# Retention and two FFNs on one core: load order of the first units, the place of float64 conversions, and two turns for background work

## The chip, the cores and the metric

One core of one Trainium2 chip runs the whole program in one launch. The metric is device microseconds of one execution; a smaller time is better. The engines are named as the profile names them: PE is TensorE (matmuls; PEld its weight loads), DVE is VectorE, ACT is ScalarE, POOL is GpSimd and SP is SyncE, which here only issues DMAs. An entry such as L456 is a line of the kernel before; in the changed kernel the same lines stand five lower in the first stage, seven lower in the next and nine lower in the last.

## The reference

The input is q, k and v (4 batches, 8 heads, 768 positions, 64 wide, float32) and two pairs of weights in float64. What is computed is a retention layer and two feed-forward networks on its 3072 tokens of width 512:

```python
for t in range(S):
    state = gamma * state + einsum('bhd,bhe->bhde', k[:, :, t], v[:, :, t])
    y[:, :, t] = scale * einsum('bhd,bhde->bhe', q[:, :, t], state)
x = y as (3072, 512)
h = x @ w_in                            # 512 -> 2048, float64 weights
x = (h * (1 / (1 + exp(-1.702 * h)))) @ w_out
h = x @ w_in2
x = (max(h, 0) ** 2) @ w_out2
```

## The kernel before, in words

**Attention stage.** The retention is cut into 24 units (4 batches by 6 chunks of 128 positions, all 8 heads). The loop at L564 to L575 runs one unit u per pass. `scores(u)` puts 16 small matmuls on PE (L456, tile `sc`), which DVE masks into `pt` (`masked`, L465); a scaled copy `vs` of v is made by POOL (L475, for u below 6 and each third unit) or by ACT (L480). `outputs(u-1)` then puts three groups on PE: `yp` (L508, needs `pt` and `vs`), `dp` (L519, the update of the state) and a second part of `yp` (L530, from the state `st`, which ACT copies at L524). DVE scales `yp` into the token blocks `x` or `xout` (`scaled`, L543, L547, L550). The tile `sc` has one buffer, so the scores of a unit wait until DVE has masked the unit before. Units 0 to 3 make block 0, whose operands `hl` ACT and DVE split at L491 and L492.

**Loads of units.** SP loads each unit in two halves of 512 KB (`load_unit`, L447): q and k laid out in pairs (columns 0 to 1024, read by the scores) and k and v by token (columns 1024 to 2048, read by `vs` and `dp`; called "kv" here). Five units have buffers. The order of the first loads is written out at L555 to L562; later, unit u+4 is asked for at the end of pass u. The small tables `tab_sb` and `ytab` lie between the first loads.

**Conversion of weights.** The first network's weights come as float64 slices of 512 KB, 32 in all. POOL's queue loads a slice into `raw` (`cv_load`, L119). ACT scales its two words (`scale_words`, called by `cv_a`; L124, L125). DVE joins them to a float32 (`join`, L129 and L134) and rounds (`round_up`, L142); ACT copies the high part (L157) and DVE subtracts for the low part (L162). `cv_step` is called once in each pass of the attention loop. It places one scaling if a slice has been asked for and fewer than two scaled ones lie ready, and a conversion in those passes that `CVU` lists; `masked` and `scaled` are put between its steps. The raw loads begin in the pass whose number the last argument of `cv_step` gives. By the end of the attention stage 9 slices are converted; the other 23 follow in the first block of the next stage.

**First network, first four blocks** (`NSTD` = 4 blocks of 512 tokens). Each block has 16 steps f; a step has `up(n, f)` (12 matmuls, L595 to L597) and `down(n, f - 2)` (12 matmuls, L626 to L628). ACT makes `gs` (L602) and its high part `gh` (L603), DVE the low part `gl` (L607), which `down` reads two steps later.

**Makers.** Once all 32 slices are converted, DVE and ACT also make the sums of weights that a seven-product form of matrix multiplication needs later. `make_first` and `make_second` are generators; `make_second` converts the 32 slices `raw2_n` of the second network (loaded by ACT's queue, L247), sums them into `w32_n`, lets ACT cast them to `wq_n` (L353) and writes each by a POOL DMA of 896 KB to `kw` in DRAM (L316). `background(us)` gives them a turn: it first drains ACT's pending pieces (`acts`), then advances the maker until the given microseconds (`BG` in the first network, `BGUP` later, with what is left over) are used up, or until it must wait for a piece of ACT.

**The rest.** The last two blocks of the first network and all of the second run as seven products (L769). SP fetches their weights as tiles `r` of 256 KB from `kw`, into 8 slots, one for each 6 matmuls. POOL loads the next operands `xb` in four DMAs of 512 KB (L641) halfway through each `up2`. The order on each engine is the order in which the program emits the work.

Of the kernel before, what the change touches and what calls it, by code (L numbers as in the profile page):

```python
# [26 lines left out]
NF = DFF // P  # L27
# [2 lines left out]
UPB = TB // P  # L30
WA = 8
LOOK = 2
WARM = 10
UNITS = 5
XHELD = 4
NL = NT // (2 * TB)
# [4 lines left out]
NSTD = 4  # L41
SLOTS = 8
EARLY = 2
BG = 4.8
CVU = (5, 8, 11, 14, 17, 20, 21, 22, 23)
RAWS = 5
BGUP = 1.8

# [9 lines left out]
def tile_retention_then_two_ffns(  # L58
# [38 lines left out]
    order = []  # L97
# [5 lines left out]
            order.append((f, 1))  # L103
    wpool = {f: wa_p for f in range(WA)}
    ws = {}
    cv = {"load": 0, "a": 0, "b": 0, "pool": None, "ahead": 3}
    cvt = {}

    def cv_load():
        n = cv["load"]  # L110
        if n == len(order):
            return
        if n >= cv["b"] + cv["ahead"]:
            return
        cv["load"] += 1
        f, s = order[n]
        raw = cv_p.tile([P, 512, 2], U32, tag="raw", name=f"raw{n}", bufs=RAWS)
        src = w1[f, :, s * 512:(s + 1) * 512].bitcast(U32)
        nc.gpsimd.dma_start(out=raw, in_=src.rearrange("p (c t) -> p c t", t=2))  # L119
        cvt[n] = raw  # L120

    def scale_words(hm, raw):

        nc.scalar.mul(hm, raw[:, :, 1].bitcast(F32), 2.0 ** -112)  # L124
        nc.scalar.mul(raw[:, :, 0], raw[:, :, 0], 2.0 ** -29)  # L125

    def join(out, hb):

        v.tensor_scalar(  # L129
            out=out, in0=hb, scalar1=3, scalar2=0x7FFFFFFF,  # L130
            op0=ALU.logical_shift_left, op1=ALU.bitwise_and,
        )
        yield
        v.scalar_tensor_tensor(  # L134
            out=out, in0=hb, scalar=0x80000000, in1=out, op0=ALU.bitwise_and, op1=ALU.bitwise_or
        )
        yield
# [6 lines left out]
    def cv_a():  # L144

        n = cv["a"]
        if n == min(cv["load"], cv["b"] + 2):
            return
        cv["a"] += 1
        scale_words(cvt[n][:, :, 1].bitcast(F32), cvt[n])  # L150

# [2 lines left out]
    def cv_high():  # L154
        if held:
            w, hm, key = held[0]
            nc.scalar.copy(out=w[:, :, 0], in_=hm.rearrange("p (k c) -> p k c", c=P))  # L157

    def cv_low():
        if held:  # L160
            w, hm, key = held.popleft()
            v.tensor_tensor(  # L162
                out=w[:, :, 1], in0=hm.rearrange("p (k c) -> p k c", c=P), in1=w[:, :, 0], op=ALU.subtract
            )
            ws[key] = w

    def cv_step(limit=len(order), f1=None, f2=None, load=True):

        n, ready = cv["b"], cv["a"]
        if cv["pool"] is not None and limit is not None:  # L170
            cv_a()
        cv_high()
        if limit is None or n >= min(limit, ready):
            for f in (f1, f2):
                if f is not None:
                    f()
            cv_low()
        else:
            cv["b"] += 1
            raw = cvt.pop(n)  # L180
            key = order[n]
            hm = cv_p.tile([P, 512], F32, tag="hm", name=f"hm{n}")
            w = wpool[key[0]].tile([P, 4, 2, P], F32R, tag=f"w{key[1]}", name=f"w{n}")
            steps = join(hm.bitcast(U32), raw[:, :, 1])
            next(steps)
            if f1 is not None:
                f1()
            next(steps)
            round_up(hm, raw)
            if f2 is not None:  # L190
                f2()
            cv_low()
            held.append((w, hm, key))
        if limit is None:
            return
        if cv["pool"] is None:
            cv_a()
        if load:
            cv_load()
            cv_load()  # L200
# [177 lines left out]
    def background(us):  # L378

        credit[0] += us  # L380
        while acts:
            acts.popleft()()
        while credit[0] > 0:
            c = next(maker, None)
            if c is None:
                credit[0] = min(credit[0], 3.0)
                return
            credit[0] -= c
# [21 lines left out]
    with tc.manual_schedule():  # L410

        with (
# [20 lines left out]
            warm = aps.tile([P, 2, NP, P], F32, tag="sc", name="warm", bufs=1)  # L433
            for i in range(WARM):
                nc.tensor.matmul(warm[:, 0, :, :], warm_sb[:, 0:P], warm_sb, start=True, stop=True)
# [5 lines left out]
            def load_unit(u, parts=(0, 1024, 2048)):  # L441
                if u >= NU:
                    return
                if u not in units:
                    units[u] = att.tile([P, 2048], F32, tag="unit", name=f"unit{u}", bufs=UNITS)
                for a, z in zip(parts, parts[1:]):
                    nc.sync.dma_start(out=units[u][:, a:z], in_=qkv[u, :, a:z])  # L447
# [106 lines left out]

            load_unit(0, (0, 512, 1024))  # L555
            nc.sync.dma_start(out=tab_sb, in_=tab)
            load_unit(1, (0, 1024))
            load_unit(0, (1024, 2048))
            load_unit(1, (1024, 2048))
            nc.sync.dma_start(out=ytab_sb[0], in_=ytab)  # L560
            for u in range(2, UNITS):
                load_unit(u)  # L562
# [1 line left out]
            for u in range(NU + 1):  # L564
                masked = scores(u) if u < NU else None
                split_0()
                scaled = outputs(u - 1) if u > 0 else None
                if 0 < u < CPB:
                    for p in range(NP):
                        nc.scalar.mul(ytab_sb[u][:, p, :], ytab_sb[0][:, p, :], ystep_sb[:, u, p:p + 1])  # L570
                if u == 18:
                    cv["ahead"] = RAWS
                cv_step(2 * WA if u in CVU else 0, masked, scaled, u >= 2)
                if u > 0:
                    load_unit(u + UNITS - 1)  # L575

# [9 lines left out]

        gs = {}
        acc = {}

        def up(n, f):  # L590
            hi, lo = weights(f, 0)
            hp = hp_p.tile([P, TB], F32, tag="h", name=f"h{n}_{f}")
            for k in range(KD):
                xh, xl = hl[n][k]
                nc.tensor.matmul(hp, lo[:, k], xh, start=(k == 0), stop=False)  # L595
                nc.tensor.matmul(hp, hi[:, k], xh, start=False, stop=False)  # L596
                nc.tensor.matmul(hp, hi[:, k], xl, start=False, stop=(k == KD - 1))  # L597
            g = g_p.tile([P, TB], F32, tag="gs", name=f"gs{n}_{f}", bufs=1)
            gh = g_p.tile([P, TB], F32R, tag="gh", name=f"gh{n}_{f}")
            gl = g_p.tile([P, TB], F32R, tag="gl", name=f"gl{n}_{f}")  # L600

            nc.scalar.activation(out=g, in_=hp, func=ACTF.Gelu_apprx_sigmoid)  # L602
            nc.scalar.copy(out=gh, in_=g)  # L603
            gs[n, f] = (gh, gl)

            def low():
                v.tensor_tensor(out=gl, in0=g, in1=gh, op=ALU.subtract)  # L607

            if n == 0 and cv["b"] < len(order):
                cv_step(len(order), None, low)  # L610
                if f % 4 < 3:
                    cv_step()
            else:
                low()
                if f < NF - 1:

                    background(BG if n < NSTD - 1 or f < 5 else BG - 1.6)

        def down(n, f):
            hi, lo = weights(f, 1)  # L620
# [9 lines left out]
        def finish(n):  # L630
            a = acc.pop(n)
            t = block_tiles(f"y{n}")
            for e in range(KD):
                (nc.scalar.copy if e % 2 else v.tensor_copy)(out=t[e // 2][:, e % 2], in_=a[e])
            for i in range(2):
                nc.gpsimd.dma_start(out=ykept[n][:, 2 * i:2 * i + 2], in_=t[i])
# [83 lines left out]
        for n in range(NSTD):  # L720
            for f in range(NF):
                up(n, f)
                if f >= LOOK:
                    down(n, f - LOOK)
                elif n > 0 and f == 0:
                    down(n - 1, NF - 1)
                    finish(n - 1)
                if f == 2 and XHELD - 2 <= n < NSTD - 2:
                    xs[n + 2] = load_block(f"x{n + 2}", xkept[n + 2])
                if n == 0 and f in (2, 3):  # L730
                    j = XHELD + f - 2
                    nc.gpsimd.dma_start(out=xkept[j], in_=xout[j])
                if n == NSTD - 1:
                    if f == 3:
                        gen = x_operands(*x_loads(*blocks[0]))
                    if f >= 5:
                        next(gen, None)
                    if f == NF - 3:
                        fetch()
            down(n, NF - 2)  # L740
            if n + 1 < NSTD:
                split_x(n + 1, xs.pop(n + 1))
# [324 lines left out]
```

## Time and profile before

| what | us |
|---|---|
| median of 3 runs | 1060.19 (1059.11 to 1060.57) |
| the profiled execution | 1059.31 |
| its span, first to last instruction | 1057.5 |
| TensorE busy in the span | 1040.0 (98%) |
| VectorE, ScalarE, GpSimd busy | 746.1, 523.5, 101.5 |
| attention stage, to the first matmul of the first network | 91.2 |
| first four blocks of the first network | 91.2 to 440 |
| seven-product part | 440 to 1053.5 |

The profile is one execution. Its own time is 1.8 us above its span (what lies before the first and after the last instruction), and 0.88 us below the median of the three runs. A page of the profile gives shares of the whole span; what a change of one stage does is read from that stage's stretch.

### The profile page before, as it was taken

Reading aid. Unit: us, or ns where it says so; the run is one execution under the profiler, and the core shown is the slowest. Engines: PE = TensorE matmul, PEld = TensorE weight load, DVE = VectorE, ACT = ScalarE, POOL = GpSimd, SP = SyncE. Lnnn points to the kernel's source line nnn. Section 1 sums busy time; section 2 is a strip of 40 time slices with the busy share of each in tenths; the row PEclk is TensorE's granted clock in tenths of the full one; section 3 lists DMA queues with packets and bytes.
Section 4 is the critical chain, followed back from the end, with each engine's and each line's share of the span. In section 5 each row is a group of like instructions: output and inputs, shape, how many; then the busy total and the mean of one; then the engine's idle time right before and its main releaser. Section 6 shows DMA issues by size and latency. Waiting matters only on the chain.

```text
span 1057.5 us, 15484 instructions
## 1 busy us (share of the span) xinstructions
PE 1040.0 (98%) x5642; PEld 859.7 (81%) x5642; DVE 746.1 (71%) x1069; ACT 523.5 (49%) x858; POOL 101.5 (10%) x147
## 2 busy tenths in 40 slices
PE   7999999999999999999999999999999999999998
PEld 5887888888888888887888888888888888888886
DVE  3889997986787869753599344888345886455953
ACT  3768774434655667554546233455233464233443
POOL 2212210111111121110000100000100000000000
PEclk9999999999999999999999999999999999999999
DMA  9996879645588687799666876667876667766664
GB/s 342 366 405 219 329 257 357 248 189 191 201 262 268 236 306 255 261 349 321 191 214 217 269 236 193 192 208 225 302 197 192 188 216 232 218 193 188 209 205 161
DMA packets 106651, 259.34 MB, mean 245 GB/s; under 512 B 11216, under 2 KB 11344, under 8 KB 106320
## 3 DMA queue, kind: packets, MB, share of 16 engines
q1 hardware_dynamic: 79088, 156.64, 46.4%
q0 software_dynamic: 22304, 83.89, 22.5%
q10 hardware_dynamic: 5184, 17.83, 4.7%
q8 instruction: 45, 0.74, 0.3%
q14 instruction: 30, 0.25, 0.1%
HBM read 184.91 MB, written 73.40 MB: 244 GB/s over the span
## 4 chain that ended last, share of the span: by engine, by line
PE 92%; DMA 5%; DVE 1%; ACT 1%; SPq 0%; issue 0%; POOL 0%; ACTq 0%; POOLq 0%; DVEq 0%
PE D L769 29%; PE X L769 16%; PE Z L769 8%; PE h L595 6%; PE y L628 6%; PE y L626 5%; PE y L627 5%; PE h L596 5%; PE h L597 5%; PE Y L769 4%; DMA r<-kw 2%; DMA unit<-qkv 2%; PE yp L508 1%; PE sc L456 1%; DMA raw<-w 1%; DVE pt L465 1%
## 5 line engine op out<-in xcount | busy, mean ns | idle before, releaser
L769 PE MATMUL D<-gx,r 128*128 128x512 f32 x1344 | 306.4, 389 | 0.0
L769 PEld LDWEIGHTS D<-gx,r 128*128 128x128 f32 x1344 | 252.1, 188 | 53.0 <-DVE gx L872 0.8
L871 ACT CAST gx<-g 128x1024 fp32r<-128x1024 f32 x112 | 116.6, 1051 | 93.1 <-PE D L769 83.5
L872 DVE TENSOR_TENSOR gx<-g,gx 128x1024 fp32r<-128x1024 f32 x112 | 136.3, 1219 | 36.9 <-ACT gx L871 36.7
L769 PE MATMUL X<-xh,r 128*128 128x512 f32 x512 | 157.9, 390 | 1.1 <-DMA r<-kw 1.0
L790 ACT COPY g<-X 128x512 f32<-128x512 f32 x96 | 56.5, 589 | 188.9 <-PE X L769 188.9
L795 DVE TENSOR_TENSOR g<-Z,g 128x512 f32<-128x512 f32 x64 | 44.2, 691 | 147.5 <-ACT g L790 101.4
L769 PEld LDWEIGHTS X<-xh,r 128*128 128x128 f32 x512 | 95.8, 188 | 22.3 <-issue 2.7
L595 PE MATMUL h<-hl,w 128*128 128x512 f32 x256 | 99.7, 389 | 0.0
L628 PE MATMUL y<-gl,w 128*128 128x512 f32 x256 | 99.7, 389 | 0.0
L769 PE MATMUL X<-xl,r 128*128 128x512 f32 x256 | 99.6, 389 | 0.0
L627 PE MATMUL y<-gh,w 128*128 128x512 f32 x256 | 99.6, 389 | 0.0
L597 PE MATMUL h<-hl,w 128*128 128x512 f32 x256 | 99.6, 389 | 0.0
L626 PE MATMUL y<-gh,w 128*128 128x512 f32 x256 | 99.6, 389 | 0.0
L596 PE MATMUL h<-hl,w 128*128 128x512 f32 x256 | 99.6, 389 | 0.0
L769 PE MATMUL Z<-xh,r 128*128 128x512 f32 x256 | 79.0, 390 | 0.7 <-DMA r<-kw 0.7
L603 ACT CAST gh<-gs 128x512 fp32r<-128x512 f32 x64 | 39.8, 622 | 72.3 <-PE y L627 71.6
L607 DVE TENSOR_TENSOR gl<-gs,gh 128x512 fp32r<-128x512 f32 x64 | 44.1, 689 | 36.6 <-ACT gh L603 36.4
L602 ACT ACTIVATE gs<-h 128x512 f32<-128x512 f32 x64 | 38.1, 595 | 48.4 <-PE h L597 39.1
L769 PEld LDWEIGHTS Z<-xh,r 128*128 128x128 f32 x256 | 47.9, 188 | 11.2 <-issue 1.1
L628 PEld LDWEIGHTS y<-gl,w 128*128 128x128 f32 x256 | 48.1, 188 | 10.4 <-DVE gl L607 0.4
L595 PEld LDWEIGHTS h<-hl,w 128*128 128x128 f32 x256 | 48.1, 188 | 10.1 <-issue 0.2
(95 smaller groups left out, 1540.4 us busy)
## 6 DMA issues: line engine op xcount, KB each, us to landing
r<-kw SPq DMA_DIRECT2D x448, 256.0 KB, 2.9
kw<-wq POOLq DMA_DIRECT2D x32, 896.0 KB, 5.8
unit<-qkv SPq DMA_DIRECT2D x47, 512.0 KB, 8.9
raw<-w POOLq DMA_DIRECT2D x32, 512.0 KB, 6.7
kw<-wh POOLq DMA_DIRECT2D x16, 1024.0 KB, 4.7
kw<-w SPq DMA_DIRECT2D x16, 512.0 KB, 7.0
raw<-win ACTq DMA_DIRECT2D x16, 512.0 KB, 5.5
raw<-wout ACTq DMA_DIRECT2D x16, 512.0 KB, 4.1
```

Source lines behind the costliest of these rows:

```text
L595: nc.tensor.matmul(hp, lo[:, k], xh, start=(k == 0), stop=False)
L596: nc.tensor.matmul(hp, hi[:, k], xh, start=False, stop=False)
L597: nc.tensor.matmul(hp, hi[:, k], xl, start=False, stop=(k == KD - 1))
L607: v.tensor_tensor(out=gl, in0=g, in1=gh, op=ALU.subtract)
L626: nc.tensor.matmul(a, lo[:, e], gh, start=s0, stop=False)
L627: nc.tensor.matmul(a, hi[:, e], gh, start=False, stop=False)
L628: nc.tensor.matmul(a, hi[:, e], gl, start=False, stop=s1)
L769: nc.tensor.matmul(a, w, b, start=start, stop=stop, skip_group_check=True)
L790: nc.scalar.copy(out=t, in_=a)
L795: v.tensor_tensor(out=t, in0=a, in1=t, op=ALU.add)
L871: nc.scalar.copy(out=hi, in_=src)
L872: v.tensor_tensor(out=lo, in0=src, in1=hi, op=ALU.subtract)
```

## The change

The changed kernel differs in four things. The kv half of unit 0 is asked for before unit 1, whose two halves follow together. A slice is scaled no earlier than four passes after its load was asked for, the loads begin one pass later, and the conversions of the attention stage stand in other passes (nine in both). `background` is called twice in each step, after `up` and after `down`, with half the microseconds each, and 4.4 a step in place of 4.8. Eight warm-up matmuls run at the start in place of ten.

```diff
-WARM = 10
+WARM = 8
...
-BG = 4.8
-CVU = (5, 8, 11, 14, 17, 20, 21, 22, 23)
+BG = 4.4
+CVU = (8, 10, 12, 13, 15, 17, 19, 21, 23)
...
     def cv_load():
...
         cvt[n] = raw
+        loaded[n] = cv["step"]
...
     def cv_a():
...
         if n == min(cv["load"], cv["b"] + 2):
             return
+        if cv["pool"] is not None and cv["step"] < loaded[n] + 4:
+            return
...
     def cv_step(limit=len(order), f1=None, f2=None, load=True):
 
+        cv["step"] += 1
...
             nc.sync.dma_start(out=tab_sb, in_=tab)
-            load_unit(1, (0, 1024))
             load_unit(0, (1024, 2048))
-            load_unit(1, (1024, 2048))
+            load_unit(1)
             nc.sync.dma_start(out=ytab_sb[0], in_=ytab)
...
-                cv_step(2 * WA if u in CVU else 0, masked, scaled, u >= 2)
+                cv_step(2 * WA if u in CVU else 0, masked, scaled, u >= 3)
...
+        def pace(n, f):
+            return (BG if n < NSTD - 1 or f < 5 else BG - 1.6) / 2
...
-                    background(BG if n < NSTD - 1 or f < 5 else BG - 1.6)
+                    background(pace(n, f))
...
                     down(n - 1, NF - 1)
                     finish(n - 1)
+                if f < NF - 1 and cv["b"] == len(order):
+                    background(pace(n, f))
```

**The order on ScalarE in the attention stage, up to the first scalings.** Before, from unit 3's pass on (`hl0` is an operand of block 0, `st` the state, `raw` a float64 slice of the first network):

```order
L524 COPY st2_324<-dp0_205 128x256
L570 ACTIVATE ytab3_131<-ytab0_128,tab_sb_127 128x128 x4
L124 ACTIVATE raw0_280<-raw0_280 128x512
L125 ACTIVATE raw0_280<-raw0_280 128x512
L491 CAST hl0_0_138<-x0_2_341 128x128
L491 CAST hl1_0_139<-x0_2_341 128x128
L491 CAST hl2_0_140<-x0_2_341 128x128
L491 CAST hl3_0_141<-x0_2_341 128x128
L524 COPY st3_385<-dp0_205 128x256
L570 ACTIVATE ytab4_132<-ytab0_128,tab_sb_127 128x128 x4
L124 ACTIVATE raw1_282<-raw1_282 128x512
L125 ACTIVATE raw1_282<-raw1_282 128x512
```

With the change, from unit 4's pass on:

```order
L529 COPY st3_379<-dp0_203 128x256
L574 ACTIVATE ytab4_132<-ytab0_128,tab_sb_127 128x128 x4
L496 CAST hl0_0_138<-x0_3_394 128x128
L496 CAST hl1_0_139<-x0_3_394 128x128
L496 CAST hl2_0_140<-x0_3_394 128x128
L496 CAST hl3_0_141<-x0_3_394 128x128
L529 COPY st4_438<-dp0_203 128x256
L574 ACTIVATE ytab5_133<-ytab0_128,tab_sb_127 128x128 x4
L485 ACTIVATE vs7_505<-unit7_339,tab_sb_127 128x64 x8
L529 COPY st6_532<-dp1_523 128x256
L126 ACTIVATE raw0_335<-raw0_335 128x512
L127 ACTIVATE raw0_335<-raw0_335 128x512
```

The scalings of `raw0` and `raw1` stood ahead of the splits of `x0_2` and `x0_3` into `hl` and the copies `st3` and `st4`; now the first scaling stands behind `st6`.

**The order on VectorE in the last of the first four blocks, between two `gl`.** Before (`w32_n` is the sum tile of slice n, `wq_n` its cast, made by ScalarE):

```order
L607 TENSOR_TENSOR gl3_2_3814<-gs3_2_3812,gh3_2_3813 128x512
L129 TENSOR_SCALAR w32_17_3824<-hm2_17_3787 128x512
L134 SCALAR_TENSOR_TENSOR w32_17_3824<-hm2_17_3787,w32_17_3824 128x512
L142 SCALAR_TENSOR_TENSOR w32_17_3824<-w32_17_3824,raw2_17_3784 128x512
L315 TENSOR_TENSOR wq_16_3798<-w32_16_3788,wq_16_3798 128x7x128
L347 TENSOR_TENSOR w32_17_3824<-w32_17_3824 128x128
L348 TENSOR_TENSOR w32_17_3824<-w32_17_3824 128x128
L350 TENSOR_TENSOR w32_17_3824<-w32_17_3824 128x128
L351 TENSOR_TENSOR w32_17_3824<-w32_17_3824 128x128
L607 TENSOR_TENSOR gl3_3_3866<-gs3_3_3864,gh3_3_3865 128x512
```

With the change:

```order
L614 TENSOR_TENSOR gl3_2_3870<-gs3_2_3868,gh3_2_3869 128x512
L136 SCALAR_TENSOR_TENSOR w32_20_3853<-hm2_20_3816,w32_20_3853 128x512
L144 SCALAR_TENSOR_TENSOR w32_20_3853<-w32_20_3853,raw2_20_3809 128x512
L320 TENSOR_TENSOR wq_19_3851<-w32_19_3817,wq_19_3851 128x7x128
L352 TENSOR_TENSOR w32_20_3853<-w32_20_3853 128x128
L353 TENSOR_TENSOR w32_20_3853<-w32_20_3853 128x128
L355 TENSOR_TENSOR w32_20_3853<-w32_20_3853 128x128
L356 TENSOR_TENSOR w32_20_3853<-w32_20_3853 128x128
L131 TENSOR_SCALAR w32_21_3905<-hm2_21_3852 128x512
L136 SCALAR_TENSOR_TENSOR w32_21_3905<-hm2_21_3852,w32_21_3905 128x512
L614 TENSOR_TENSOR gl3_3_3923<-gs3_3_3921,gh3_3_3922 128x512
```

Eight maker instructions stood between these two `gl`, and nine do now; the maker is three slices further on, `wq_19` is read behind two instructions of slice 20 instead of three, and slice 21 is begun in the same step.

**The order on GpSimd's queue at the end of the first four blocks.** Before (`ykept` takes the last block's result, `kw` the makers' sums, `xb` the next operands):

```order
L636 DMA ykept3_116<-y3_0_4501 128x1024
L636 DMA ykept3_116<-y3_1_4502 128x1024
L316 DMA kw115_108<-wq_27_4426 128x7x256
L316 DMA kw116_109<-wq_28_4582 128x7x256
L316 DMA kw116_109<-wq_29_4707 128x7x256
L316 DMA kw117_110<-wq_30_4791 128x7x256
L641 DMA xb1_0_0_0_4874<-ykept0_113 128x1024
L641 DMA xb1_0_0_1_4875<-ykept0_113 128x1024
L641 DMA xb1_0_1_0_4878<-ykept1_114 128x1024
L641 DMA xb1_0_1_1_4879<-ykept1_114 128x1024
L316 DMA kw117_110<-wq_31_4873 128x7x256
```

With the change:

```order
L643 DMA ykept3_116<-y3_0_4531 128x1024
L643 DMA ykept3_116<-y3_1_4532 128x1024
L321 DMA kw116_109<-wq_29_4470 128x7x256
L321 DMA kw117_110<-wq_30_4651 128x7x256
L321 DMA kw117_110<-wq_31_4761 128x7x256
L648 DMA xb1_0_0_0_4876<-ykept0_113 128x1024
L648 DMA xb1_0_0_1_4877<-ykept0_113 128x1024
L648 DMA xb1_0_1_0_4880<-ykept1_114 128x1024
L648 DMA xb1_0_1_1_4881<-ykept1_114 128x1024
```

Behind the two stores of `y3`, five writes of `kw` were left, four of them ahead of the loads of `xb`; three are left now, all ahead of `xb`.

## Rows read from the trace of the kernel before

**Rows 1.** The page: the engines' busy time, and one row of the DMA issues.

```profile
PE 1040.0 (98%) x5642; PEld 859.7 (81%) x5642; DVE 746.1 (71%) x1069; ACT 523.5 (49%) x858; POOL 101.5 (10%) x147
...
r<-kw SPq DMA_DIRECT2D x448, 256.0 KB, 2.9
```

**Rows 2.** Stretches of the span: length, busy us (instructions) of each engine, granted clock, DMA, GB/s.

```profile
10.00:20.00 10.00, 7.71 (x124) 6.85 (x122) 4.92 (x10) 4.58 (x18) 5.89 (x7) 0.83 1.01 397
20.00:32.00 12.00, 9.32 (x161) 8.33 (x160) 7.89 (x18) 7.10 (x23) 2.61 (x3) 0.86 1.02 410
32.00:45.00 13.00, 12.90 (x252) 11.28 (x252) 10.98 (x20) 8.79 (x29) 3.60 (x4) 1.00 0.93 324
45.00:80.00 35.00, 34.45 (x668) 30.25 (x666) 30.54 (x48) 24.62 (x84) 7.00 (x9) 1.00 1.02 405
80.00:91.20 11.20, 9.38 (x197) 7.97 (x192) 10.91 (x16) 9.99 (x29) 2.03 (x3) 1.00 0.79 302
91.20:440.00 348.80, 348.80 (x1541) 288.51 (x1538) 294.28 (x529) 203.20 (x323) 55.14 (x75) 1.00 0.72 252
440.00:500.00 60.00, 57.97 (x251) 46.30 (x250) 27.37 (x50) 30.92 (x53) 7.63 (x11) 1.00 0.96 340
500.00:1053.50 553.50, 553.46 (x2439) 457.14 (x2437) 357.08 (x381) 232.79 (x301) 17.29 (x32) 1.00 0.70 212
```

**Rows 3.** Waits of TensorE, 0 to 91 us: total us, times, longest.

```profile
PE sc L456 <- DVE pt L465: 3.9, 4, 2.7
PE sc L456 <- DMA unit<-qkv: 3.7, 3, 2.8
```

**Rows 4.** Timeline, 0 to 13 us: start, us, instruction, idle before it and releaser.

```profile
9.24 1.16 PE L456 MATMUL sc<-unit 64*128 64x128 f32 x16 [2.83 <-DMA unit<-qkv]
...
10.90 2.22 POOL L475 TENSOR_TENSOR vs<-unit,tab_sb 128x512 f32<-128x512 f32 x2 [10.04 <-DMA unit<-qkv]
...
11.99 1.33 PE L508 MATMUL yp<-pt,vs 128*64 128x128 f32 x10 [1.59 <-POOL vs L475]
```

**Rows 5.** Timeline, 24 to 33 us.

```profile
24.30 0.68 ACT L124 ACTIVATE raw<-raw 128x512 f32<-128x512 f32 x1 [1.28 <-DMA raw<-w]
...
25.43 0.88 ACT L491 CAST hl<-x 128x128 fp32r<-128x128 f32 x4
...
27.82 1.50 PE L456 MATMUL sc<-unit 64*128 64x128 f32 x16 [2.68 <-DVE pt L465]
```

**Rows 6.** Stretches: from one unit's scores to the next unit's, twice.

```profile
27.82:32.59 4.77, 4.76 (x64) 4.28 (x65) 4.01 (x9) 2.26 (x8) 1.42 (x3) 0.64 1.03 411
41.23:44.41 3.18, 3.18 (x68) 2.82 (x65) 2.44 (x4) 0.42 (x2) 1.58 (x2) 1.00 0.97 344
```

**Rows 7.** The chain that ended last: start, us, what.

```profile
72.78 10.34 DMA unit<-qkv
...
481.48 11.88 DMA r<-kw
```

**Rows 8.** Groups of VectorE by line and shape, 32 to 91 us: busy us, mean ns.

```profile
L142 DVE SCALAR_TENSOR_TENSOR hm<-hm,raw 128x512 uint16<-128x512 uint16 x9 | 6.8, 759 | 0.3
L134 DVE SCALAR_TENSOR_TENSOR hm<-raw,hm 128x512 uint32<-128x512 uint32 x9 | 6.3, 697 | 0.0
L162 DVE TENSOR_TENSOR w<-hm,w 128x512 fp32r<-128x512 f32 x7 | 4.8, 688 | 1.6 <-ACT w L157 1.5
...
L129 DVE TENSOR_SCALAR hm<-raw 128x512 uint32<-128x512 uint32 x8 | 3.4, 419 | 0.1
```

**Rows 9.** Waits of TensorE, 440 to 500 us.

```profile
PE X L769 <- DMA r<-kw: 1.0, 3, 0.5
```

**Rows 10.** DMA issues, 474 to 493 us: count, KB each, median us to landing.

```profile
r<-kw SPq DMA_DIRECT2D x12, 256.0 KB, 9.7
...
kw<-wq POOLq DMA_DIRECT2D x2, 896.0 KB, 9.0
```

**Rows 11.** A group of ScalarE, 340 to 440 us: busy us, mean ns.

```profile
L353 ACT CAST wq<-w 128x896 fp32r<-128x896 f32 x14 | 13.1, 937 | 3.3 <-DVE w L351 3.3
```

More of the change, by code (lines that the diff above doesn't have):

```diff
@@ L105, in tile_retention_then_two_ffns @@
     ws = {}
-    cv = {"load": 0, "a": 0, "b": 0, "pool": None, "ahead": 3}
+    cv = {"load": 0, "a": 0, "b": 0, "pool": None, "ahead": 3, "step": 0}
+    loaded = {}
     cvt = {}
```

## The prediction

> **What bounds the kernel now.** I read the page first: TensorE is busy for 1040.0 us, 98% of the span of 1057.5 [rows 1], so all that can be won without removing matmuls is 17.5 us, and the table of stretches [rows 2] shows where it lies. The first four blocks of the first network (91.2 to 440) and the part behind 500 us are full: 348.80 of 348.80 and 553.46 of 553.50. Most of what is idle behind the first loads lies in the attention stage (2.29 us in 10 to 20, 2.68 in 20 to 32, 0.10 + 0.55 + 1.82 up to 91.2: 7.4 in all) and at the start of the seven-product part (2.03 in 440 to 500). The same table shows what limits the attention stage: the DMA share stands at 1.01 to 1.02 from 10 to 32 and from 45 to 80 us, at 397 to 410 GB/s, and only 32 to 45 has room (324 GB/s). The largest waits of TensorE there [rows 3] are 3.9 us for `pt` and 3.7 for a unit's load; what lies behind the first is in the timeline [rows 5], ScalarE standing for a `raw` slice.
>
> The sum goes against the profiled execution, 1059.31 us, which is 0.88 below the median of 1060.19. The kernel's measurement can tell about 0.2%, or 2.1 us, from no change.
>
> **Start: the load order and two warm-up matmuls, 0.** Unit 0's kv and unit 1's qk are equally large and change places. So `vs` of unit 0, which began at 10.90, can begin near 9.24, and the scores of unit 1, which began at 9.24, begin near 10.90 [rows 4]. They take 1.16 us at full clock and end at about 12.1. TensorE's next work, `yp` of unit 0, stood for `vs` until 11.99 [rows 4]; it now finds `vs` ready and follows at 12.1. The order of the two waits changes and the sum doesn't: one wait of 1.6 goes, and one of 2.83 grows by 1.66. The other end is a lower clock: TensorE is then idle from 6.4 (9.24 - 2.83) to 10.9 without a break, and the granted clock of 10 to 20 us is 0.83 already [rows 2]. Scores at half clock would take another 1.2 us. The low end is 0, since the scores can't precede their load. Two warm-up matmuls fewer lie in the time before unit 0's first load is there; their price is nothing, or a part of that same 1.2. I take 0, as the 10 to 20 us behind are set by the loads (share 1.01), whose bytes don't change; range 0 to +1.3.
>
> **Scalings out of the way of units 4 and 5: -4.0 at that place.** Up to now they stand ahead of the splits into `hl` (the first listing). ScalarE stands 1.28 us for `raw` and so reaches the splits into `hl` only at 25.43; without the wait and the scaling it is free at 24.30 - 1.28 = 23.02, or 2.4 us earlier. VectorE's split and mask are behind it, and behind them the scores of unit 5, which TensorE waited 2.68 for [rows 5]. So -2.4. The granted clock fell behind that wait: the step from scores to scores took 4.77 us at a mean clock of 0.64, and the same four groups at 1.00 took 3.18 [rows 6]. If the wait goes, so does this: -1.6. Together -4.0 by unit 6.
>
> **Given back to the transfers: +2.7.** A unit that is worked off 4.0 us earlier must have landed 4.0 us earlier. Loads already run at 405 to 410 GB/s from 10 to 32 and from 45 to 80 [rows 2], so an earlier request doesn't make them land earlier there. Room lies only in 32 to 45: 13 x (405 - 324) / 405 = 2.6 us. The loads of slices begin one pass later but the conversions are denser, so that at the last unit's load one more slice has been asked for than before: 524288 bytes at 405 GB/s are 1.3 us. What can be kept is 2.6 - 1.3 = 1.3 us, so 4.0 - 1.3 = 2.7 goes back, as waits for `unit`. That the end hangs on loads already is in the chain: a unit's load of 10.34 us from 72.78 is its last long piece in the stage [rows 7]. Ends: 0 given back (if loads can run faster when asked earlier), and all 4.0.
>
> **Denser conversions: +1.0.** Passes 8 to 17 hold six conversions in place of four. One costs VectorE 0.42 + 0.70 + 0.76 + 0.69 = 2.56 us [rows 8], the two some 5.1. VectorE has 35 - 30.54 = 4.5 us idle in 45 to 80 [rows 2], which is 4.0 in the 31 us that ten passes take, so 1.1 is left over; I take +1.0. Ends: 0 where they fall into waits for loads, +2 where half of the idle time lies in the wrong passes.
>
> **End of the stage: -0.3.** Three conversions stand in the last four passes where four stood. VectorE is busy 10.91 of 11.20 us there [rows 2], so one less shortens its queue, but `vs` of the last unit is ready hardly before `pt`. Ends 0 and -1.0.
>
> Attention in all: -4.0 + 2.7 + 1.0 - 0.3 = **-0.6**, ends -4.0 and +1.5 (nothing given back to loads; all of it, with +1.3 at the start and less for the conversions).
>
> **First four blocks, 0.** TensorE has no idle time there that could be won. The two turns make each step's work for the makers lie in two pieces; VectorE executes it between the same two `gl` as before (the second listing: eight instructions, now nine), and `gl` is read two steps later. The cover is that distance; what happens when it is gone is a rival below.
>
> **Fetches of the seven-product part: -1.7.** The idle 2.03 us of 440 to 500 [rows 2] are waits for `r` (the group of X is half of them [rows 9]), whose loads take 9.7 us from issue to landing in 474 to 493 [rows 10] against 2.9 as the median over the kernel [rows 1]; the chain runs through one of 11.88 us there [rows 7]. Two writes of `kw` (896 KB each) fall in that stretch [rows 10], beside the four loads of `xb`. With the change three writes are left behind the last stores in place of five (the third listing), all ahead of `xb`; so the two in that stretch are gone, 1.8 MB beside the 3.1 MB of `r` asked for there (12 of 256 KB). Behind 500 us, where the later loads of `xb` meet no such write, TensorE is idle for 0.04 us in 553.50 [rows 2]. The three writes that stay still fall ahead of it, so I leave one wait of X's mean, 1.0 / 3 = 0.3 [rows 9], and take the rest as gone: -1.7. Ends: -2.0, and 0 if the loads of `xb` alone are enough to hold up `r`.
>
> Sum: -0.6 + 0 - 1.7 = -2.3; 1059.31 - 2.3 = 1057.0 for that execution, and 1060.19 - 2.3 = **1057.9** against the median.
>
> **The rivals.**
> (A+) *Loads follow.* If loads asked for earlier do land earlier, nothing is given back: -4.0 - 0.3 + 0 - 1.7 = -6.0, or 1054.2. For it: 410 GB/s in 20 to 32 is above the 405 of 45 to 80. Against it: a share of 1.02 has no idle engine.
> (B) *The loads are a floor.* The time from 10 to 80 us is set by bytes, the room of 32 to 45 is used up by slices, and attention gains 0: only -1.7, or 1058.5. For it: the share; against it: 2.6 us of room.
> The Trainium skill, in "DMA: Bandwidth & Descriptors", section "Specifications", gives an HBM limit of about 358 GB/s for one core. By that figure, as an estimate, the 27.3 MB that the rows from 10 to 80 us show moved would take 76 us in place of 70, the stage would have no room at all, and this rival's 1058.5 would be the time. The trace disagrees: 405 GB/s stand for 35 us on end [rows 2], so I give the rival no more for it.
> (C) *Fetch waits stay.* `xb` alone holds `r` up: -0.6, or 1059.6. Against it stands the idle 0.04 behind 500 us.
> (D) *VectorE becomes the bound in the last of the four blocks, slower.* It is busy for 294.28 of the 348.80 us of the four blocks [rows 2]; a step is 348.8 / 64 = 5.45 us, so 0.85 a step is free. With two turns, a piece that ScalarE got in the first is taken up in the second, so that VectorE can stand for ScalarE's cast of 0.94 us [rows 11] in each turn, 1.88 a step, where a whole step lay between before. It decides once the waits pass 0.85 a step: 1.88 - 0.85 = 1.03 us in each of the six steps before f = 6, where nine instructions lie between two `gl`, is +6.2, and with -2.3 it is +3.9, or 1064.1. Against it: the listing still has instructions of another slice between such pairs, and `gl` has two steps of time.
> (E) *The start loses.* +1.3 there, +2 for the conversions, all 4.0 given back: attention +3.0, and +1.3 in all, or 1061.5; over 1062.3 only if the fetch waits stay too.
>
> **How the numbers follow.** Forecast 0.50, A+ 0.11, B 0.17, C 0.08, D 0.08, E 0.06. The forecast lies near the bound of 2.1 us; of its 0.50 I put 0.34 beyond it, as the extremes of its attention term reach further down than up. Faster: 0.34 + 0.11 = 0.45; same: 0.16 + 0.17 + 0.08 + 0.02 of E = 0.43; slower: 0.08 + 0.04 = 0.12. The range 1054.8 to 1061.5 takes in B, C, most of E and part of A+, and leaves out D and the rest of A+.
>
> **What would show it.** Right: the scores of unit 1 begin near 10.9 and `yp` behind them without a wait; no wait of ScalarE for `raw` ahead of unit 6, and no fall of the clock there; longer waits of TensorE for `unit` behind it; the first matmul of the first network near 90.6 in place of 91.2; 348.8 us for the four blocks; hardly a wait for `r` behind 474. Wrong: an attention stage that ends over 2 us earlier or at all later, a wait for `gl` in the four blocks, or waits for `r` of over 1 us in 474 to 500.

## The result and the profile after

The changed kernel takes 1068.88 us (1066.21 to 1071.06, 6 runs) against 1059.65 of the kernel before: a ratio of 1.0088, 95% interval 1.0070 to 1.0106, or 9.2 us slower. Its profiled execution took 1067.7 us, with a span of 1065.9 against 1057.5. First the page (first line and engines), as in [rows 1]:

```profile
span 1065.9 us, 15474 instructions
...
PE 1041.4 (98%) x5640; PEld 858.5 (81%) x5640; DVE 744.9 (70%) x1069; ACT 524.3 (49%) x858; POOL 101.1 (9%) x147
```

TensorE's work is the same within 1.4 us; 8.4 us of span were added. Where, the same stretches as in [rows 2] say; the limits of the last three are moved to the first matmul of the first network and to that of the seven-product part:

```profile
10.00:20.00 10.00, 8.65 (x132) 7.84 (x134) 4.91 (x10) 4.57 (x18) 4.44 (x6) 0.83 1.01 398
20.00:32.00 12.00, 11.12 (x224) 9.55 (x222) 9.61 (x21) 6.41 (x25) 4.27 (x6) 1.00 0.98 364
32.00:45.00 13.00, 11.32 (x216) 10.23 (x218) 8.13 (x15) 9.55 (x30) 1.58 (x2) 1.00 1.03 405
45.00:80.00 35.00, 31.06 (x607) 26.87 (x602) 33.07 (x52) 25.62 (x85) 7.62 (x11) 1.00 1.01 395
...
92.12:450.30 358.18, 351.50 (x1539) 287.45 (x1538) 297.22 (x542) 206.80 (x327) 57.61 (x77) 1.00 0.73 254
450.30:510.00 59.70, 59.28 (x261) 48.46 (x260) 22.17 (x37) 27.93 (x48) 5.82 (x9) 1.00 0.89 299
```

The four blocks have grown from 348.6 us to 358.2. Before, TensorE was busy in every one of them; now it is busy for 351.50 of 358.18. (The busy time itself grew by 2.9 us: behind each of the five waits below, the first few matmuls start 0.33 to 0.53 us apart, where 0.23 is the mean before.) The sum of the three parts, by the starts of the first matmul `h` and of the first `X`:

| part | before | after | difference |
|---|---|---|---|
| attention stage | 91.22 | 92.06 | +0.84 |
| first four blocks | 348.59 | 358.21 | +9.62 |
| seven-product part, with what follows | 617.72 | 615.66 | -2.06 |
| span | 1057.53 | 1065.93 | +8.40 |

The waits of TensorE over the whole span (us, times, longest), which answer to [rows 3] and [rows 9]:

```profile
PE sc L461 <- DMA unit<-qkv: 5.8, 3, 3.7
PE y L633 <- ACT gh L610: 5.0, 4, 1.8
PE sc L461 <- DVE pt L470: 4.8, 8, 1.0
PE h L602 <- ACT hl L411: 1.5, 1, 1.5
...
PE X L778 <- DMA r<-kw: 0.7, 2, 0.5
...
PE Z L778 <- DMA r<-kw: 0.2, 1, 0.2
```

Two of them lie in the four blocks, where there was none before: 5.0 us for `gh` and 1.5 for `hl`, both made by ScalarE. ScalarE itself is busy for only 206.80 of 358.18 us there, and so stands for something. Its waits in 270 to 345 us, in the changed kernel:

```profile
ACT hm L126 <- DMA raw<-win: 20.9, 11, 4.1
...
ACT wq L358 <- DMA kw<-wq: 4.5, 3, 2.3
```

and in the kernel before:

```profile
ACT gh L603 <- PE y L627: 24.8, 13, 1.9
...
ACT hm L124 <- DMA raw<-win: 1.8, 5, 0.9
```

Before, ScalarE's time without work went to waiting for TensorE, which is no loss; a slice `raw` cost it 1.8 us. Now it stands 20.9 us for eleven landings. The timeline of ScalarE shows how (ACTq is its queue of DMA issues):

```profile
275.46 0.33 ACTq L252 DMA_DIRECT2D raw<-win  x1
275.90 0.60 ACT L609 ACTIVATE gs<-h 128x512 f32<-128x512 f32 x1 [0.56 <-DVE w L144]
...
282.88 0.67 ACT L126 ACTIVATE hm<-raw 128x512 f32<-128x512 f32 x1 [4.11 <-DMA raw<-win]
...
288.66 0.67 ACT L126 ACTIVATE hm<-raw 128x512 f32<-128x512 f32 x1 [2.53 <-DMA raw<-win]
...
293.84 0.66 ACT L126 ACTIVATE hm<-raw 128x512 f32<-128x512 f32 x1 [1.97 <-DMA raw<-win]
...
315.31 0.62 ACT L610 CAST gh<-gs 128x512 fp32r<-128x512 f32 x1
315.31 0.34 ACTq L252 DMA_DIRECT2D raw<-win  x1
317.62 0.95 ACT L358 CAST wq<-w 128x896 fp32r<-128x896 f32 x1 [1.69 <-DVE w L356]
320.36 0.66 ACT L126 ACTIVATE hm<-raw 128x512 f32<-128x512 f32 x1 [1.79 <-DMA raw<-win]
...
321.47 0.57 ACT L609 ACTIVATE gs<-h 128x512 f32<-128x512 f32 x1
322.07 0.62 ACT L610 CAST gh<-gs 128x512 fp32r<-128x512 f32 x1
322.08 0.33 ACTq L252 DMA_DIRECT2D raw<-win  x1
...
327.62 0.67 ACT L126 ACTIVATE hm<-raw 128x512 f32<-128x512 f32 x1 [2.29 <-DMA raw<-win]
...
343.30 0.58 ACT L609 ACTIVATE gs<-h 128x512 f32<-128x512 f32 x1
```

There are two parts. The first is a late load: asked for at 275.46, it took 7.39 us, and though a gelu stands between (L609 at 275.90), the scaling at 282.88 had waited 4.11 us, with the next `gs` behind it. ScalarE was then late, and the next scalings stood for their loads as well (2.53 and 1.97 us, then less). The second part, from 315 on, is in the written order. `gh` of one step begins and a slice is asked for (both at 315.31), ScalarE casts one `wq`, and then the scaling of that same slice is next: 1.79 us of standing up to 320.36, 2.29 up to 327.62. Only behind the scaling comes the gelu of the next step (321.47), and only with its `gh` the next load (322.08). So a step takes a whole landing and the gelu one after the other: from load to load 6.77 us (315.31 to 322.08), where TensorE needs 5.45. From the `gs` at 275.90 to the one at 343.30 lie ten steps in 67.4 us, 12.9 more than ten of TensorE's. The parts weigh about the same: of the 20.9 us of standing, 11.3 are at six slices with a gelu between load and scaling and 9.6 at five without; six steps up to the `gs` at 314.69 are 6.1 us longer than TensorE's, the four behind it 6.8.

The same engine in the kernel before:

```profile
303.55 0.62 ACT L603 CAST gh<-gs 128x512 fp32r<-128x512 f32 x1 [1.95 <-PE y L627]
304.08 0.66 ACT L124 ACTIVATE hm<-raw 128x512 f32<-128x512 f32 x1
304.13 0.34 ACTq L247 DMA_DIRECT2D raw<-win  x1
304.64 0.68 ACT L125 ACTIVATE raw<-raw 128x512 uint32<-128x512 uint32 x1
305.21 0.92 ACT L353 CAST wq<-w 128x896 fp32r<-128x896 f32 x1
306.44 0.60 ACT L602 ACTIVATE gs<-h 128x512 f32<-128x512 f32 x1 [0.31 <-PE h L597]
308.99 0.62 ACT L603 CAST gh<-gs 128x512 fp32r<-128x512 f32 x1 [1.95 <-PE y L627]
309.79 0.67 ACT L124 ACTIVATE hm<-raw 128x512 f32<-128x512 f32 x1 [0.18 <-DMA raw<-win]
```

Here a load (304.13) goes out with the scaling of the slice before it, and the next step's `gs` (306.44) and `gh` (308.99) lie between it and its own scaling, which waits 0.18 us. The load takes 5.6 us here too; but ScalarE does its gelu while it runs. The written order shows the difference without a profile. In the changed kernel, between two steps of the third block:

```
L610 CAST gh2_8_3376<-gs2_8_3375 128x512
L252 DMA raw2_12_3381<-win2 128x1024
L358 CAST wq_10_3387<-w32_10_3341 128x7x128
L126 ACTIVATE hm2_12_3388<-raw2_12_3381 128x512
L127 ACTIVATE raw2_12_3381<-raw2_12_3381 128x512
L609 ACTIVATE gs2_9_3423<-h2_9_3410 128x512
```

The order runs like this for slices 11 to 16: of the two turns between two gelus, the first drains a slice's load and the second its scaling. In the chain of the changed kernel the loads follow one another:

```profile
275.46 7.39 DMA raw<-win
282.94 5.69 DMA raw<-win
288.72 5.10 DMA raw<-win
...
322.08 5.52 DMA raw<-win
329.36 5.00 DMA raw<-win
336.11 6.06 DMA raw<-win
```

Before, the chain ran through no load between 92 and 440 us. TensorE has a cover of two steps, 10.9 us, and loses nothing at first; here it is used up:

```profile
328.75 0.57 ACT L609 ACTIVATE gs<-h 128x512 f32<-128x512 f32 x1
329.35 0.62 ACT L610 CAST gh<-gs 128x512 fp32r<-128x512 f32 x1
...
330.02 0.50 PE L633 MATMUL y<-gh,w 128*128 128x512 f32 x1 [0.90 <-ACT gh L610]
```

`y` stands 0.90 us for a `gh` that ended at 329.97.

### The profile page after: what moved, and what is told of

Read it like the earlier page. It is cut to its first block, busy times and chain, and to the rows that moved or that the text cites. A ratio compares the mean times of both kernels' runs of the same rounds, so it can differ in the third digit from the quotient of the medians.

```text
span 1065.9 us, 15474 instructions
## 1 busy us (share of the span) xinstructions
PE 1041.4 (98%) x5640; PEld 858.5 (81%) x5640; DVE 744.9 (70%) x1069; ACT 524.3 (49%) x858; POOL 101.1 (9%) x147
## 4 chain that ended last, share of the span: by engine, by line
PE 82%; DMA 10%; DVE 4%; ACT 2%; issue 1%; SPq 1%; ACTq 0%; DVEq 0%
PE D L778 29%; PE X L778 15%; PE Z L778 8%; DMA raw<-win 5%; PE h L604 4%; PE h L602 4%; PE h L603 4%; PE y L635 4%; PE y L633 4%; PE y L634 4%; PE Y L778 4%; DMA unit<-qkv 3%; DMA r<-kw 2%; DVE pt L470 1%; PE sc L461 1%
## 5 line engine op out<-in xcount | busy, mean ns | idle before, releaser
L633 PEld LDWEIGHTS y<-gh,w 128*128 128x128 f32 x256 | 48.0, 188 | 16.3 <-ACT gh L610 6.6
L602 PEld LDWEIGHTS h<-hl,w 128*128 128x128 f32 x256 | 48.1, 188 | 11.9 <-ACT hl L411 2.0
L604 PEld LDWEIGHTS h<-hl,w 128*128 128x128 f32 x256 | 48.0, 188 | 10.8 <-DVE hl L412 0.8
```

Of the source, the lines that this page charges most:

```text
L633: nc.tensor.matmul(a, lo[:, e], gh, start=s0, stop=False)
```

## The experiments

A theory (L) and rivals stood behind the first four runs. L: the second turn drains ScalarE's pieces, so loads and scalings of a slice meet with no gelu between. V: two turns fill VectorE (the prediction's rival D). P: the attention stage did it.

**Two turns alone** (`turns_alone`): the kernel before with these lines of the change.

```diff
-BG = 4.8
+BG = 4.4
...
-                    background(BG if n < NSTD - 1 or f < 5 else BG - 1.6)
+                    background(pace(n, f))
...
+                if f < NF - 1 and cv["b"] == len(order):
+                    background(pace(n, f))
```

> The kernel before with the two turns and 4.4 us a step alone; attention stage as before. Theory L (slices 11 to 16 of the makers are asked for and scaled with no gelu between, so ScalarE stands 2 to 4 us for each landing in front of the next gelu): first four blocks 6 to 9 us longer, seven-product part 1 to 2 us shorter, so 1064 to 1068. Rival V (VectorE itself is full, from its waits for ScalarE's casts): the same time, so this run doesn't part L and V. Rival P (most of the loss comes from the attention stage and reaches the blocks through the state in which it leaves the weights): 1057 to 1060, no ScalarE wait for raw of over 2 us.

Measured: 1066.58 us, ratio 1.0078 (1.0062 to 1.0093). The four blocks take 357.3 us, the rest 2.1 less than before. ScalarE's wait for slices in 270 to 345 us:

```profile
ACT hm L124 <- DMA raw<-win: 20.0, 11, 3.5
```

The blocks' 8.7 us are nearly all of the loss, and P is out. Not all of the standing is at slices without a gelu between, as L had it: in the changed kernel 11.3 of the 20.9 us are not.

**The attention part alone** (`att_alone`): the changed kernel with one turn.

```diff
-BG = 4.4
+BG = 4.8
...
-                    background(pace(n, f))
+                    background(BG if n < NSTD - 1 or f < 5 else BG - 1.6)
...
-                if f < NF - 1 and cv["b"] == len(order):
-                    background(pace(n, f))
```

> The changed kernel with one turn of 4.8 us a step, so the attention part (load order, lag of 4, passes of the conversions, 8 warm-up matmuls) alone. Theory L and rival V: four blocks of 348.8 us without a wait, the attention stage 0.5 to 2 us longer, so 1060 to 1062. Rival P: 1065 or more.

Measured: 1060.36 us, 1.0011 (1.0001 to 1.0021); the blocks take 348.3 us without a wait. The attention part costs about 1 us (0.1 to 2.2).

**Two turns, but one drain** (`one_drain`): the changed kernel, in which the second turn leaves ScalarE's pieces alone.

```diff
-    def background(us):
+    def background(us, drain=True):
...
-        while acts:
+        while drain and acts:
...
-                    background(pace(n, f))
+                    background(pace(n, f), False)
```

> The changed kernel, both turns kept, but the second turn doesn't drain ScalarE's pending pieces. Every load of a maker slice then has a gelu between it and its scaling. Theory L: four blocks back to 348.8 us, no wait of the blocks' matmuls; the writes of the makers are again as late as before, so the fetch waits of up to 2 us return: 1060 to 1062. Rival V (two turns fill VectorE): still 1065 or more, as VectorE's work and its split into two turns are unchanged.

Measured: 1058.82 us, 0.9994 (0.9985 to 1.0003). That is faster than the 1060 to 1062 expected: the part behind the blocks was 0.9 us shorter than before, not as long. The blocks are back at 348.3 us, and ScalarE hardly waits:

```profile
ACT hm L126 <- DMA raw<-win: 2.3, 4, 1.0
```

VectorE still has its two turns, though the makers get less far in them; V falls here, and with the makers as far on as in the changed kernel in sp_load, below.

**Scalings held back** (`late_scale`): both turns drain, but a scaling waits in the list until two turns behind its load.

```diff
...
-        while acts:
-            acts.popleft()()
+        turns[0] += 1
+        for _ in range(len(acts)):
+            run, n = acts.popleft()
+            if n is not None and turns[0] < turn_of[n] + 2:
+                acts.append((run, n))
+            else:
+                run()
```

> The changed kernel, both turns drain, but a scaling of a maker slice is drained no earlier than two turns behind its load. Theory L: ScalarE's waits for raw fall from 21 us in 270 to 345 us to under 5, four blocks at 348.8, fetch waits under 1 us: 1059 to 1061. Rival V: VectorE's work is the same and its waits for ScalarE no shorter: 1065 or more.

Measured: 1057.61 us, 0.9992 (0.9982 to 1.0002). The profiled execution took 1062.36 us, with the blocks at 352.4, so L's number for the blocks was missed in it; ScalarE stood 8.6 us for slices in 270 to 345, where under 5 was expected, and the time came out below the range given. The profile shows a second place, in the last block, where four loads of `xb` share the queues with the slices. ScalarE in 384 to 398 us of that kernel:

```profile
384.05 0.66 ACT L126 ACTIVATE hm<-raw 128x512 f32<-128x512 f32 x1 [4.43 <-DMA raw<-wout]
...
391.57 0.67 ACT L126 ACTIVATE hm<-raw 128x512 f32<-128x512 f32 x1 [4.31 <-DMA raw<-wout]
```

Those waits end in one of TensorE for `gh`, 2.2 us. So holding back the scaling by two turns is not enough in every execution.

**4.2 us a step** (`bg42`): the changed kernel, one number changed; the order then has a gelu between load and scaling for slices 11 to 16.

```diff
-BG = 4.4
+BG = 4.2
```

> The changed kernel with 4.2 in place of 4.4 us a step; both turns and all else kept. In the order on ScalarE the six slices 11 to 16 then again have a gelu between load and scaling (only slices 2, 30 and 31 have none). Theory L: four blocks back to 348.5 to 350 us; five writes of kw are left behind the last stores, so the fetch waits of about 2 us return; 1059 to 1062. A rival V2, that two turns as such cost ScalarE or VectorE time in each step: 0.2 us of 4.4 can't undo it, 1065 or more.

Measured: 1062.94 us, 1.0030 (1.0013 to 1.0047), just outside what L gave, with a wide spread: 1056.89 to 1067.08 over twelve runs. The profiled one took 1059.86, its blocks 348.3 us; but ScalarE's wait for slices was not small even there:

```profile
ACT hm L126 <- DMA raw<-win: 13.0, 7, 4.7
```

Its loads of slices follow one another too, but without a burst ScalarE made its delay good: the waits end at 313 us. Two turns as such (V2) would have shown in every run. What makes others take up to 7 us longer has no profile and stays open.

**4.6 us a step** (`turns46`), on the kernel before: shorter bursts.

```diff
-BG = 4.4
+BG = 4.6
```

> The kernel before with two turns and 4.6 us a step: bursts of three (slices 11 to 13) and two (22, 23) slices without a gelu between load and scaling, in place of a burst of six. Theory L: ScalarE falls about 5 us behind with the first and 1.3 more with each further slice, up to some 10 us behind at the end of three, where two steps of 5.45 are the cover: 0 to 2 us of waits of TensorE in the four blocks; no write of kw is left behind the last stores, so the seven-product part gains 2 us: 1057 to 1060. V2: 1065 or more.

Measured: 1067.22 us, 1.0078 (1.0066 to 1.0090): a miss, the blocks took 358.5 us. I had worked from the burst alone. The waits lie in two places, at the change from the third block to the last (2.0 us for `hl`, 1.0 behind it, 0.8 for `gl`) and in the last block (1.7 for `gh`), where ScalarE stands for slices beside `xb`, here in 365 to 405 us:

```profile
ACT hm L124 <- DMA raw<-wout: 10.2, 4, 5.4
```

Of these 10.2 us, 4.1 are at two slices without a gelu between (22 and 23) and 5.4 at one that has it, whose load took 9.3 us. So the count of slices without a gelu between was not enough to tell the size.

**4.6 us a step with the scalings held back** (`late46`), on the kernel before: the edit of late_scale on turns46.

> The kernel before (its attention stage kept) with two turns, 4.6 us a step, and no scaling drained earlier than two turns behind its load. Theory L: four blocks 348.6 us, fetch waits under 0.8 us; 1056.5 to 1058. V2: 1065 or more.

Measured: 1057.80 us, 0.9989 (0.9979 to 0.9999); blocks 348.6, the rest 2.0 us shorter than before. ScalarE in 270 to 345 us:

```profile
ACT hm L124 <- DMA raw<-win: 3.6, 4, 2.1
```

turns46, with the same turns and the same 4.6 us a step, took 9.4 us more, so V2 falls too.

**Eight conversions** (`late46_eight`): late46 with the changed attention stage, one conversion less in it.

```diff
-CVU = (8, 10, 12, 13, 15, 17, 19, 21, 23)
+CVU = (8, 10, 12, 14, 16, 18, 20, 22)
```

> As late46, but with the changed attention stage and eight conversions in it at passes 8, 10, 12, 14, 16, 18, 20, 22; the ninth goes to the first of the four blocks, where weights are ready 9 us or more ahead. If the changed stage's length is set by VectorE (33.1 us busy of 35 in 45 to 80), one conversion of 2.5 us less shortens it by 1 to 2.5 us against the changed kernel's 92.1: 89.5 to 91, and 1055 to 1057.5 in all. If loads set it, it stays near 92 and the time at 1057.5 to 1059.

Measured: 1058.41 us, 0.9991 (0.9980 to 1.0002). The stage ended at 90.48 in place of 92.06 (91.18 to 93.70 in the six profiles of the changed stage), but the blocks took 350.3 (TensorE waited 1.0 us for `gh` in the last one), and the time didn't move. VectorE is still busy for 33.53 us of 45 to 80:

```profile
45.00:80.00 35.00, 31.40 (x599) 27.53 (x600) 33.53 (x52) 25.38 (x82) 6.76 (x9) 1.00 1.02 397
```

So a shorter stage is there, and is not shown to be a gain.

**Slices asked for by SyncE** (`sp_load`): the changed kernel, the load moved instead of the scaling.

```diff
-            nc.scalar.dma_start(out=raws[n], in_=src.rearrange("p (c t) -> p c t", t=2))
+            nc.sync.dma_start(out=raws[n], in_=src.rearrange("p (c t) -> p c t", t=2))
...
-                later(lambda n=n: load(n + 2))
+                load(n + 2)
```

> The changed kernel with the makers' float64 slices asked for by SyncE's queue right behind the rounding that frees their buffer, in place of by ScalarE at the next turn; turns, 4.4 us a step and scalings as changed. Theory L: a slice is asked for some half step (2 to 3 us) earlier, so ScalarE's waits for raw in 270 to 345 us fall from 21 to under 8, and the four blocks to 349 to 351: 1057.5 to 1061. V2 (two turns as such): 1065 or more.

Measured: 1058.40 us, 0.9986 (0.9977 to 0.9995): faster than the kernel before by 1.5 us and than the changed one by some 10. Blocks 348.3 us, no wait of TensorE in them. ScalarE in 270 to 345 us:

```profile
ACT hm L126 <- DMA raw<-win: 5.2, 3, 3.4
```

The turns, their microseconds and the place of each scaling are those of the changed kernel; only the load comes earlier, and on SyncE's queue. ScalarE's other waits were not what cost the time: in the same stretch it stood 10.5 us for VectorE's `w` and 3.7 for the writes of `kw`, against 6.4 and 4.5 in the changed kernel, and TensorE lost nothing. With late46 it is the version that beats both kernels, by an amount near what can be told.

**The same at 4.6, with xb two steps earlier** (`sp46x`), attention stage of before. The edit beside those of turns46 and sp_load:

```diff
-                    if f == 3:
+                    if f == 1:
                         gen = x_operands(*x_loads(*blocks[0]))
```

> The attention stage of before, two turns of together 4.6 us, slices asked for by SyncE as in sp_load, and the loads of xb in the last of the four blocks two steps earlier (step 1 in place of 3). If turns46 lost its time by ScalarE standing for slices, and in the last block for slices that share the queues with xb: four blocks 348.5 to 350, the seven-product part 611.8, 1056 to 1058.5. If two turns at 4.6 us are too much for VectorE: 1063 or more, as turns46.

Measured: 1058.51 us, 0.9991 (0.9980 to 1.0002); blocks 348.6 us in the profile, where turns46 took 358.5. The two edits were not tried apart.

**The load order alone** (`order_only`), on the kernel before.

```diff
-            load_unit(1, (0, 1024))
             load_unit(0, (1024, 2048))
-            load_unit(1, (1024, 2048))
+            load_unit(1)
```

> The kernel before with unit 0's kv ahead of unit 1 alone. By the prediction's step: the waits of 2.83 and 1.59 us become one of 4.2 to 4.5, and the end of the stage doesn't move by more than 0.5 us: 1058.6 to 1059.8. If the order itself costs: the stage 1 us or more longer, 1060.2 or more.

Measured: 1059.49 us, 1.0003 (0.9993 to 1.0013): no change, as the prediction's step had it. The scores of unit 1 began at 9.96 behind one wait of 3.2 us, a shorter one than the 4.2 to 4.5 expected, with no wait of `yp` for `vs`, and the stage ended at 91.58.

**Lag and passes of the conversions alone** (`lag_only`), on the kernel before.

```diff
-CVU = (5, 8, 11, 14, 17, 20, 21, 22, 23)
+CVU = (8, 10, 12, 13, 15, 17, 19, 21, 23)
...
+        if cv["pool"] is not None and cv["step"] < loaded[n] + 4:
+            return
...
-                cv_step(2 * WA if u in CVU else 0, masked, scaled, u >= 2)
+                cv_step(2 * WA if u in CVU else 0, masked, scaled, u >= 3)
```

> The kernel before with the lag of four passes, loads from pass 3 and the changed passes of conversions alone. If VectorE's denser conversions carry the loss of the attention stage: TensorE idle over 2.5 us in 45 to 80, but no fall of the clock ahead of unit 6; stage 0.5 to 1.5 us longer: 1060 to 1061. If not: 1058.5 to 1059.5.

Measured: 1058.43 us, 0.9995 (0.9983 to 1.0007), so the time came out as the second case said. But the profile shows the first case's mechanism. The stretch 45 to 80 us:

```profile
45.00:80.00 35.00, 31.02 (x598) 26.86 (x600) 32.91 (x51) 25.60 (x84) 7.13 (x10) 1.00 1.02 395
```

TensorE is idle for 4.0 us there, against 0.55 in [rows 2]; the same stretch of order_only, where the conversions stand as before:

```profile
45.00:80.00 35.00, 33.73 (x654) 29.50 (x652) 31.16 (x47) 24.59 (x84) 6.27 (x8) 1.00 1.01 391
```

In lag_only's profiled execution (1062.32 us, stage 93.25) that is a loss; how much of the idle time survives to the end in others isn't settled: by the runs, between -1.8 and +0.7 us.

## Why the prediction was wrong, step by step

- **First four blocks, 0: the step that failed.** It said that VectorE executes the two pieces "between the same two `gl` as before", and took the distance of `gl` as the cover. The listing of VectorE was read rightly; VectorE was not where the change worked. The second turn also drains ScalarE's pieces, and by that it moves loads and scalings of slices against the gelu, which the listing of ScalarE would have shown (the excerpt above). The sign named for this step, a wait for `gl`, did not appear; TensorE waited 5.0 us for `gh` and 1.5 for `hl`, which ScalarE makes. Measured: +9.6 us. turns_alone gives it without the rest of the change, one_drain and sp_load take it away with the turns kept.
- **Rival D had the sign, a chance of 0.08 and the wrong engine.** VectorE is 83% busy in the blocks (297.22 of 358.18), no more than before. The time of 1064.1 was short by 4.8 us.
- **Start, 0: right.** One wait of 3.7 us until 10.62, `yp` behind it without a wait; order_only: 1.0003. The lower clock named as the other end did come: the scores at 10.62 ran at a granted 0.50 and took 2.08 us. It cost nothing, as the scores of unit 2 began at 14.76 where they began at 14.75.
- **Scalings out of the way, -4.0 at that place: right.** No wait for `raw` ahead of unit 6, whose scores began at 28.51 in place of 32.59, 4.1 us earlier; the granted clock of 20 to 32 us is 1.00 where it was 0.86, and TensorE is busy for 11.12 us there in place of 9.32.
- **Given back to the transfers, +2.7: about right.** Waits for `unit` of 1.27 and 0.85 us appear at 32.6 and 36.1, and 32 to 45 now runs at 405 GB/s in place of 324, as the room of 2.6 us said. The Trainium skill's limit in "DMA: Bandwidth & Descriptors", section "Specifications", is about 358 GB/s; the trace is above it in one more stretch, at 405.
- **Denser conversions, +1.0 (ends 0 and +2): too small.** TensorE's idle time in 45 to 80 us went from 0.55 to 3.94 us, +3.4, with VectorE at 33.07 of 35. All of it is waits for `pt`, which stands in VectorE's queue with the conversions: 2.5 of the 4.5 us that VectorE had idle were filled, and `pt` came late. How the loss divides between this term and the one before isn't firm: in lag_only's profile no wait for `unit` is left behind 28 us.
- **End of the stage, -0.3: misread and too small.** The passes 20 to 23 hold two conversions (21 and 23) and not three. TensorE's idle time behind 80 us went from 1.82 to 0.74 us.
- **Attention in all, -0.6: the sign was wrong.** +0.84 in the profile and +1.1 (0.1 to 2.2) by att_alone, where the ends were -4.0 and +1.5. Single executions differ more: the changed stage ended at 91.18 to 93.70 us in six profiles, that of before at 91.22 to 91.70 in five.
- **Fetches, -1.7: right.** -2.06; the waits for `r` between 474 and 500 are 0.42 us, with three writes of `kw` left. Seven profiles with two draining turns take 615.6 to 615.9 us from the first `X` to the end (bg42 and sp46x, where less is done early or `xb` moved, 616.4 and 616.7); four with one turn take 617.7 to 619.2.

The sum without the failed step is -1.2 (0.84 - 2.06) in the profile. sp_load, which undoes that step alone, measured 1.5 us below the kernel before.

## What to carry to other kernels

Where a change gives an in-order engine its pieces at more places, list that engine's order, and look for each DMA and its first reader: what matters is what stands between them, counted in the time of a landing, and what stands behind the reader. Here a cover of two steps took up one late landing (bg42's profile), and not one late landing and six slices behind it without work between load and reader (the changed kernel). To ask for the data earlier, on a queue with nothing urgent behind it, was worth the whole loss here.

## What the runs showed of the hardware

A DMA that stood behind computing instructions in ScalarE's order did not wait for the last of them to run. In the kernel before, the load at 304.13 us stands behind both words of the scaling; it went out 0.05 us after the first began and 0.51 before the second (304.64). And the first loads didn't land alike: with the load order and the conversions of before, the scores of unit 1 began at 9.24, 8.19, 8.50, 8.86 and 8.00 us in five profiled executions (before, turns_alone, turns46, late46, sp46x), and the stage ended between 91.22 and 91.70.
